# A convolution by transforms woven with a mixture of experts: gate operations spread over a step and held at the turn, spare x tiles handed out earlier, output transposes moved behind the next kind's first matmuls

## The chip, the cores and the metric

The kernel runs on one NeuronCore of a Trainium2 chip. The engines are TensorE (PE; PEld is its weight load), VectorE (DVE), ScalarE (ACT), GpSimd (POOL) and SyncE (SP). Each takes its own instructions in program order; SP, ACT and POOL also issue DMAs. The metric is the device time of one execution in microseconds (us).

## The reference, cut to what matters

```python
Xf = np.fft.rfft(x, n=2*S, axis=1); Hf = np.fft.rfft(h, n=2*S, axis=0)
y = np.fft.irfft(Xf * Hf[None], n=2*S, axis=1)[:, :S, :]     # 8 x 5056 x 128
x = y.reshape(B * S, D)
g = argmax(x @ w_group); e = argmax(x @ w_expert[g])         # 4 groups of 4 experts
out = g_w * e_w * (relu(x @ w1[g, e]) @ w2[g, e])            # F = 1024; softmax weights of the two choices
```

Every one of 8 x 5056 tokens of 128 channels is convolved along its sequence, and the result is routed to one of 16 experts.

## The kernel before, in words

**Three rounds of the convolution.** Round 0 transforms h and two sequences of x, rounds 1 and 2 three sequences each. A round has three stages. *Stage 1* (`stage1`, 96 half steps over 48 x tiles) multiplies an x tile by the matrix `f` on PE; ACT and DVE evacuate to `st`. Matmuls read x tiles from five permanent tiles `xt` and, later in the round, from four tiles `xy` that are the idle product tiles (tag `y`), zeroed by POOL in `clear` (L387). When tile i is done its buffer is free again and up to two loads (`load`, L402) are issued, from SP in round 0 and from ACT's queue in rounds 1 and 2. *Groups* (`groups`, 20 double steps a round): a step does two forward transforms (PE L520), for each two products from PSUM on DVE (`y` and `m`, L538), their sum (L572, POOL in round 0, DVE after), and two inverse transforms of the step before (PE L588), evacuated by ACT (`zs`, L598) and stored to `zd`. Forward, inverse and stage 1 take turns on three PSUM buffers `pp`. *Side* (`side`): round r's last stage and its gates run beside the later round: lumps of last transform (PE L722, L736 on `zm`, `zt` loaded from `zd`), logits (`lm`, L789; `lt`, L799), transposes of rows (`rows`, L779, evacuated by ACT as `rw`, L780), then `gate_math` on DVE (some 33 small operations, eight empty turns, and a last part with two pairs of small matmuls L972, L973, then `off`, `base`, `cs`, `posf`, L976 to L986), and scatters of rows by POOL (L855), each preceded by a cast of `pos`.

**The weave.** `run` writes rounds 0 to 2 and the experts' steps as one list `main` of (weight, function). `weave` runs it in order and lays each side's steps between by weight. A group step has eleven entries, `GW = [0, 0, 0, 0, 0, 0, 2.0, 0, 0, 0, 2.0]`, so side work falls due at its seventh and eleventh entry. A side's large steps run where they fall due. Small ones (gate operations) wait in `light` and are flushed at entries of weight 0, evenly over the run of zeros at hand (`room`): the six at a step's start or the three between the two weights. One eighth of a side takes eight units of its own time: lumps at 0 and 3, `lm` with the first rows at 4.7, `lt` with the next at 6.4, the rest of the rows (`more`) at 9.5, gate operations from 6.5 to 12.1.

**The turn and the experts.** After round 2's groups `turn` gives the PSUM and SBUF of the transforms to the experts; `ffn_first` transposes the first block's rows (L1306) and splits them and the first weights into high and low parts (L1298 on ACT, L1299 on DVE). Each block of tokens is then eight steps of `mm1` (L1351 to L1353; ACT's relu L1356, DVE's low part L1357) and `mm2` (L1369 to L1371). Round 2's last inverses stand between the first experts' steps. Blocks come in three kinds, of 512, 384 (`T0`) and 256 (`H0`) tokens; the later ones hang on counts that are known at run time (branches at L1555). Between kinds the kernel does two `mm1` of the next kind, then `ffn_drain`: the last two `mm2`, `out_evac` (ACT, `oT`, L1374), transposes of `oT` (PE, L1385), the scaled rows (DVE, L1389) and the scatter (POOL, L1422).

Of the kernel before, what the change touches and what calls it, by code (L numbers as in the profile page):

```python
# [20 lines left out]
N1, N2 = 158, 64  # L21
L = N1 * N2
NH = S // N2
# [3 lines left out]
BLK = 512  # L27
# [9 lines left out]
TB, HB = 384, 256  # L37
# [12 lines left out]
SLOTS = 56  # L50
LATE = 4
END0 = 20
SIDEG = 8
NTA = 7
FILL = 12
AHEAD = 40
# [114 lines left out]
    }  # L171


def weave(main, sides):


    light = []

    def flush(n):
        for f in light[:n]:  # L180
            f()
        del light[:n]

    room = [0] * (len(main) + 1)
    for i in reversed(range(len(main))):
        room[i] = room[i + 1] + 1 if main[i][0] == 0 else 0
    for i, (w, f) in enumerate(main):
        f()
        if w == 0:
            flush(-(-len(light) // room[i]))  # L190
        for s in sides:
            if s["start"] <= i < s["end"]:
                if i == s["start"]:
                    s["done"] = 0
                    s["acc"] = s["sacc"] = 0.0
                    s["len"] = sum(w for w, _ in main[s["start"]:s["end"]])
                    s["total"] = sum(x[0] for x in s["steps"])
                s["acc"] += w / s["len"]
                while s["done"] < len(s["steps"]) and (s["sacc"] < s["acc"] * s["total"] - 1e-6 or i == s["end"] - 1):
                    sw, sf, small = s["steps"][s["done"]]  # L200
                    if small and room[i + 1] > 0 and i < s["end"] - 1:
                        light.append(sf)
                    else:
                        if small:
                            flush(len(light))
                        sf()
                    s["sacc"] += sw
                    s["done"] += 1
                if i == s["end"] - 1:
                    flush(len(light))  # L210
# [18 lines left out]
class Kernel:  # L229
# [33 lines left out]
    def setup(self):  # L263
        nc, a, cp, dr = self.nc, self.a, self.cp, self.dr
        self.zd = [dr.tile([N1, N2, W], F32, name=f"zd{r}") for r in range(3)]
        self.hd = dr.tile([NQ, 128, 2, D], F32, name="hd")
        self.outd = dr.tile([PUT1 - PUT0, 128, 2, D], F32, name="outd")
        self.puts, self.taken = [], []
        self.srt = dr.tile([NR, ROW], F32, name="srt")
        self.tabd = [dr.tile([128, 2], I32, name=f"tabd{i}") for i in range(6)]  # L270

        self.xt = [cp.tile([128, 512], F32, name=f"xt{i}") for i in range(XT)]
        for t in self.xt:
            nc.vector.memset(t, 0.0)
        self.f = cp.tile([128, N1], F32, name="f")
        nc.sync.dma_start(out=self.f, in_=a["c_f"])

# [93 lines left out]
    def stage1(self, r):  # L371
# [21 lines left out]
        def load(eng=nc.sync):  # L393
            if asked[0] >= len(loads) or not free:
                return
            i = asked[0]
            asked[0] += 1
            u, q = loads[i]
            b = ROUNDS[r][u]
            src = a["h"] if b < 0 else a["x"][b]  # L400
            held[i] = t = free.pop(0)
            eng.dma_start(  # L402
                out=t[X0:X0 + NH + 1].rearrange("p (d n) -> p d n", n=N2), in_=src[:, 2 * q * QB:2 * (q + 1) * QB, :]
            )
            tiles[i] = t.rearrange("p (i h n) -> p i h n", h=2, n=N2)

        def mm(k):
# [34 lines left out]
            else:  # L442
                nc.scalar.copy(out=all_st[:, :, d], in_=whole.rearrange("p (i j) -> p j i", i=QB)[:, 0:N1])
            free.append(held.pop(i))
            c = i - (5 if r > 0 else 0)
            if 0 <= c < 4:
                clear()
            if 2 <= c < 6:
                free.append(cleared[c - 2])
            for _ in range(2):  # L450
                load(nc.scalar if r > 0 else nc.sync)

# [232 lines left out]
    def side(self, r):  # L685
# [131 lines left out]
        for o in range(N2 // 8):  # L817
            math = {}
            ops = self.gate_math(od, math, b0 * S + o * 8, T, nu, REST if r < 2 else REST2)
            sends = [self.scatter(math, k, GP if k < T - 1 else last, r, T) for k in range(T)]  # L820
            if r < 2:
                t = 8 * o
                at.append((t, lump(2 * o), False))
                at.append((t + 3, lump(2 * o + 1), False))
                at.append((t + 4.7, both(lm, lambda: rows(0)), False))
                at.append((t + 6.4, both(lt, lambda: rows(1)), False))
                at.append((t + 9.5, both(*more), False))
                at += [(t + 6.5 + 5.6 * k / (NMATH + REST), advance(ops), True) for k in range(NMATH + REST)]
                at.append((t + 12.15, lambda o=o, s=sends: self.sends.extend((8 * r + o, f) for f in s), True))
            else:  # L830

                t = 6 * o
                at.append((t, lump(2 * o), False))
                at.append((t + 2, lump(2 * o + 1), False))
                at.append((t + 3, both(lm, lambda: rows(0)), False))
                at.append((t + 4, both(lt, lambda: rows(1)), False))
                at.append((t + 5, both(*more), False))
                at += [(t + 4.02 + 3.3 * k / (NMATH + REST2), advance(ops), True) for k in range(NMATH + REST2)]
                at.append((t + 7.4, lambda o=o, s=sends: self.sends.extend((8 * r + o, f) for f in s), True))
# [701 lines left out]

        return [step(i) for i in range(ns)]

    def ffn_drain(self, n):
        ns = steps_of(n)
        self.mm2(n, ns - 2, 0)
        self.mm2(n, ns - 1, 0)
        self.out_evac(n, 0)
        self.out_store(n, self.lids)
        self.scatter_out(4)  # L1550

# [26 lines left out]
    def ffn_tail(self):  # L1578
# [4 lines left out]
        nt = nc.values_load(self.nbt, min_val=0, max_val=NE)  # L1583
        nh = nc.values_load(self.nbh, min_val=0, max_val=NE)
        self.ffn_chain(NW_MIN, NW_MAX, nw, NC, (BLK, self.lids))
        for i in range(2):
            self.mm1(T0, i)
        self.ffn_drain(BLK)
        self.no_rows()
        self.ffn_chain(T0, T0 + NE, nt, T0, None)  # L1590
        for i in range(2):
            self.mm1(H0, i)
        self.ffn_drain(TB)
        self.no_rows()
        self.ffn_chain(H0, H0 + NE, nh, H0, None)
        self.ffn_drain(HB)
# [1 line left out]
    def run(self):  # L1598
        tc = self.tc
        with ExitStack() as ctx:  # L1600
            self.pools(ctx)
            with ExitStack() as c2:
# [29 lines left out]
                for r in range(3):  # L1632
# [27 lines left out]
                    for p in range(0, NQ, 2):  # L1660
                        for w, f in steps[p // 2]:
                            add(f, w)
                        if p >= NQ - LOAD1:
                            add(advance(s1[r + 1][0] if r < 2 else early))
                add(turn)
                add(lambda: self.ffn_first(0))
                rest = late(2)
# [3 lines left out]
                for k, f in enumerate(steps):  # L1671
# [22 lines left out]
                    if k < 4:  # L1694
                        add(lambda q=(0, 2, 1, 3)[k]: self.ffn_w(1, (q,)))
                    add(f, FW[k % 8])
                    if k in (8 * (N0 - 2) - 1, 8 * (NA - 2) - 1):
                        add(self.drain)
                    elif k < 8 * (NA - 2) and k % 8 not in (3, 4, 5, 6):
# [7 lines left out]
                        add(lambda i=m * n // TAKE: self.take(i))  # L1707
                weave(main, [
                    dict(start=mark["start", r], end=mark["end", r], steps=side[r][1]) for r in range(3)
                ])  # L1710
                self.ffn_tail()


# [25 lines left out]
```

## Time and profile before

| | us |
|---|---|
| median of 3 runs | 1701.14 (1698.09 to 1708.59) |
| the profiled execution | 1700.13 |
| its span, first to last instruction | 1698.3 |
| PE busy in the span | 1630.5 (96%) |
| DVE, ACT, POOL busy | 1302.5, 1046.8, 773.3 |
| granted PE clock, mean | 0.991 |

The profiled execution's time is 1.8 us more than its span. The parts of the profile used below are the busy times by stretch, the waits (an engine's idle time before an instruction, put down to what came last), the timeline (start, length, engine, line, operation, idle time before it and who ended it), the groups of instructions by line, and the DMA queues (q1 is SP's, q10 is ACT's). Matmuls are pipelined, so a busy PE is not PE at its peak. A granted clock of 1 is 2.4 GHz, of 0.5 is 1.2 GHz.

### The profile page before, as it was taken

What the parts mean: (1) busy time and instruction counts of PE and PEld (TensorE: products, weight loads), DVE (VectorE), ACT (ScalarE), POOL (GpSimd) and SP (SyncE); (2) the same over time, 40 slices, a digit from 0 to 9 for tenths busy, and PEclk for the clock granted to TensorE, in tenths of its full rate; (3) what the DMA queues carried; (4) which work ended last, traced back from release to release, by engine and by line L of the source; (5) the groups of instructions that cost most, each with busy time, mean ns of one, the idle gap of its engine ahead of it and who ended that gap; (6) DMA issues with size and microseconds to landing.
All of it is one profiled execution on the core that took longest, in us unless ns stands there. A gap on an engine that the chain in (4) does not pass through costs nothing. (4 is left out here: it accounts for less than half of the span.)

```text
span 1698.3 us, 50924 instructions
## 1 busy us (share of the span) xinstructions
PE 1630.5 (96%) x18317; PEld 1275.8 (75%) x18317; DVE 1302.5 (77%) x3092; ACT 1046.8 (62%) x2461; POOL 773.3 (46%) x742
## 2 busy tenths in 40 slices
PE   8998999989899989999999999999999999999996
PEld 7676755557665557888778887888888888879986
DVE  6554698975788886777777788888887787878875
ACT  5564544544545456666666676777777776657764
POOL 1452233442555553254554454446565663334443
PEclk9999999999999999999999999999999999999998
DMA  7797678888798976566655544567555774444554
GB/s 210 224 295 223 191 243 263 274 245 217 200 289 280 287 227 172 165 177 179 177 164 173 158 139 129 153 197 219 161 161 152 213 220 139 126 132 145 164 160 139
DMA packets 278001, 330.36 MB, mean 195 GB/s; under 512 B 31863, under 2 KB 210304, under 8 KB 277720
## 3 DMA queue, kind: packets, MB, share of 16 engines
q1 hardware_dynamic: 248856, 270.93, 54.6%
q0 software_dynamic: 20608, 41.79, 7.2%
q10 hardware_dynamic: 8256, 14.10, 3.0%
q8 instruction: 152, 2.49, 0.7%
q14 instruction: 129, 1.06, 0.2%
HBM read 230.35 MB, written 96.86 MB: 193 GB/s over the span
## 5 line engine op out<-in xcount | busy, mean ns | idle before, releaser
L855 POOL DMA_INDIRECT srt<-rw,pos x320 | 345.3, 1079 | 391.4 <-DVE pos L854 116.2
L1422 POOL DMA_INDIRECT out<-orow,at x176 | 187.8, 1067 | 254.1 <-ACT at L1420 226.8
L1422 POOL DMA_INDIRECT out<-orow,sids x92 | 94.1, 1022 | 126.1 <-DVE orow L1389 89.4
L538 DVE TENSOR_TENSOR y<-pp,hg 128x768 f32<-128x768 f32 (+1 forms) x120 | 103.6, 864 | 54.3 <-ACT hg L528 32.3
L598 ACT COPY zs<-pp 128x768 f32<-128x768 f32 (+1 forms) x118 | 85.3, 723 | 81.0 <-PE pp L588 40.5
L588 PE MATMUL pp<-y,cg 64*64 64x384 f32 (+1 forms) x1472 | 116.4, 444 | 12.1 <-DVE m L538 8.0
L1357 DVE SCALAR_TENSOR_TENSOR h0l<-px,h0h 128x512 fp32r<-128x512 f32 (+1 forms) x109 | 73.7, 676 | 59.3 <-ACT h0h L1356 58.4
L520 PE MATMUL pp<-st,cg 64*64 64x192 f32 (+1 forms) x1556 | 114.4, 404 | 1.2 <-PE pp L520 0.6
L1356 ACT ACTIVATE h0h<-px 128x512 fp32r<-128x512 f32 (+1 forms) x109 | 63.9, 587 | 80.6 <-PE px L1353 72.5
L438 DVE TENSOR_TENSOR st<-pp,odd 128x320 f32<-128x320 f32 x96 | 46.9, 489 | 77.2 <-ACT odd L437 76.9
L538 DVE TENSOR_TENSOR m<-pp,hg 128x768 f32<-128x768 f32 (+1 forms) x120 | 102.9, 857 | 2.1 <-ACT hg L530 2.1
L1357 DVE SCALAR_TENSOR_TENSOR h2l<-px,h2h 128x512 fp32r<-128x512 f32 (+1 forms) x112 | 75.5, 674 | 31.0 <-ACT h2h L1356 29.9
L588 PEld LDWEIGHTS pp<-y,cg 64*64 64x64 f32 x1472 | 55.4, 133 | 52.4 <-issue 27.6
L722 PEld LDWEIGHTS py<-ig,zm 126*64 126x64 f32 x2048 | 75.0, 139 | 24.6 <-issue 8.2
L743 ACT COPY yT<-py 128x474 f32<-128x474 f32 (+1 forms) x96 | 44.3, 514 | 77.3 <-PE py L736 70.9
L1357 DVE SCALAR_TENSOR_TENSOR h3l<-px,h3h 128x512 fp32r<-128x512 f32 (+1 forms) x111 | 74.6, 672 | 22.5 <-ACT h3h L1356 21.0
L722 PE MATMUL py<-ig,zm 126*64 126x79 f32 x2048 | 83.2, 237 | 8.0 <-DMA zm<-zd 4.7
L520 PEld LDWEIGHTS pp<-st,cg 64*64 64x64 f32 x1556 | 59.0, 133 | 41.1 <-issue 32.5
L572 POOL TENSOR_TENSOR y<-y,m 128x512 f32<-128x512 f32 x40 | 50.8, 1274 | 76.8 <-DVE m L560 43.3
L1356 ACT ACTIVATE h3h<-px 128x512 fp32r<-128x512 f32 (+1 forms) x111 | 65.3, 588 | 29.1 <-PE px L1353 24.4
L1357 DVE SCALAR_TENSOR_TENSOR h1l<-px,h1h 128x512 fp32r<-128x512 f32 (+1 forms) x111 | 74.7, 673 | 4.2 <-ACT h1h L1356 0.3
L1356 ACT ACTIVATE h1h<-px 128x512 fp32r<-128x512 f32 (+1 forms) x111 | 65.2, 587 | 17.0 <-PE px L1353 14.6
(476 smaller groups left out, 5151.7 us busy)
## 6 DMA issues: line engine op xcount, KB each, us to landing
wr<-in_moe_w SPq DMA_DIRECT2D x373, 256.0 KB
zd<-zs SPq DMA_DIRECT2D x78, 384.0 KB
zm<-zd SPq DMA_DIRECT2D x64, 378.0 KB
cg<-in_c_g SPq DMA_DIRECT2D x102, 224.0 KB
xr<-srt SPq DMA_DIRECT2D x71, 260.0 KB
hg<-hd SPq DMA_DIRECT2D x80, 128.0 KB
zd<-zs SPq DMA_DIRECT2D x39, 256.0 KB
xt<-in_x ACTq DMA_DIRECT2D x54, 160.0 KB
```

The costliest lines, as they stand in the source:

```text
L438: nc.vector.tensor_tensor(out=all_st[:, 0:2 * HALF, d], in0=even, in1=odd, op=ALU.add)
L520: nc.tensor.matmul(px[c * 64:c * 64 + 64, b, to], lhsT=k, rhs=data[:, of], start=begin, stop=i == len(steps) - 1 or p == 0 and i == 1, til ...
L538: nc.vector.tensor_tensor(out=t[:, :, 0:w].rearrange("p t (r u d) -> p t r u d", r=2, u=nu), in0=taken(px, part).unsqueeze(1).broadcast_to ...
L572: (nc.gpsimd if r == 0 else nc.vector).tensor_tensor(out=y[:, :, 0:w], in0=y[:, :, 0:w], in1=m[:, :, 0:w], op=ALU.add)
L588: nc.tensor.matmul(pz[c][h:h + 64, 0:w], lhsT=wt[c * 64:c * 64 + 64, k + h:k + h + 64], rhs=y[c * 64:c * 64 + 64, part, 0:w], start=part = ...
L598: nc.scalar.copy(out=z[:, 0:n, 0:w], in_=pp[:, 0:n, 0:w])
L722: nc.tensor.matmul(pys[q][c:c + 64, col(n, u)], lhsT=zms[q][:, n % QB, k:k + 64], rhs=self.ig[:, 0:NH], start=n % QB == 0 and u == 0, stop ...
L743: nc.scalar.copy(out=self.yT[:, k:k + QB * c1], in_=pys.pop(q)[:, 0:QB * c1])
L855: ins = self.nc.gpsimd.indirect_dma_start(out=self.srt, out_offset=bass.IndirectOffsetOnAxis(ap=k["pos"][0:p, j:j + 1], axis=0), in_=k["rw ...
L1356: nc.scalar.activation(out=hh, in_=p, func=AF.Relu)
L1357: nc.vector.scalar_tensor_tensor(out=hl, in0=p, scalar=0.0, in1=hh.bitcast(F32), op0=ALU.max, op1=ALU.subtract)
L1422: ins = self.nc.gpsimd.indirect_dma_start(out=self.a["out"], out_offset=bass.IndirectOffsetOnAxis(ap=ids, axis=0), in_=o, in_offset=None, ...
```

## The change

Six edits:

- `weave`: over the convolution a zero entry's `room` is the number of zeros among the next eleven entries (nine in a group step) when that is over five, so that light operations are shared out over a whole step. From five entries ahead of `turn` to the end of the experts' second step (`hold`) none is flushed, and those that fall due are kept.
- The side's schedule in rounds 0 and 1: `lt` from 6.4 to 5.8, `more` from 9.5 to 7.4, gate operations from 6.5 to 5.9.
- Round 0's side starts two half steps of stage 1 later (`SIDEG` 8 to 10). Round 1's start stays, since `END0` is 20.
- In rounds 1 and 2 the four product tiles are zeroed at x tiles 0 to 3 and handed out at 2 to 5; before it was 5 to 8 and 7 to 10.
- The first x tile's zeroing and load are cut in two halves.
- Between kinds of blocks the two `mm1` of the next kind stand after `out_evac` and before the transposes of `oT`.

```diff
-SIDEG = 8
+SIDEG = 10
...
-def weave(main, sides):
+def weave(main, sides, turn, start):
...
+    hold = range(turn - 5, start)
+    for i in range(turn):
+        near = sum(w == 0 for w, _ in main[i:min(i + len(GW), turn)])
+        room[i] = near if near > len(GW) // 2 else room[i]
     for i, (w, f) in enumerate(main):
         f()
-        if w == 0:
+        if w == 0 and i not in hold:
             flush(-(-len(light) // room[i]))
...
-                    if small and room[i + 1] > 0 and i < s["end"] - 1:
+                    if small and (room[i + 1] > 0 or i in hold) and i < s["end"] - 1:
                         light.append(sf)
...
         for t in self.xt:
-            nc.vector.memset(t, 0.0)
+            for c in (slice(0, 256), slice(256, 512)) if t is self.xt[0] else (slice(0, 512),):
+                nc.vector.memset(t[:, c], 0.0)
...
+            n = 2 if r == 0 and i == 0 else 1
+            for c in range(n):
+                d = slice(2 * q * QB + 2 * QB // n * c, 2 * q * QB + 2 * QB // n * (c + 1))
...
-            c = i - (5 if r > 0 else 0)
-            if 0 <= c < 4:
+            if i < 4:
                 clear()
-            if 2 <= c < 6:
-                free.append(cleared[c - 2])
+            if 2 <= i < 6:
+                free.append(cleared[i - 2])
...
-                at.append((t + 6.4, both(lt, lambda: rows(1)), False))
-                at.append((t + 9.5, both(*more), False))
-                at += [(t + 6.5 + 5.6 * k / (NMATH + REST), advance(ops), True) for k in range(NMATH + REST)]
+                at.append((t + 5.8, both(lt, lambda: rows(1)), False))
+                at.append((t + 7.4, both(*more), False))
+                at += [(t + 5.9 + 5.6 * k / (NMATH + REST), advance(ops), True) for k in range(NMATH + REST)]
...
-    def ffn_drain(self, n):
+    def ffn_drain(self, n, following=None):
         ns = steps_of(n)
         self.mm2(n, ns - 2, 0)
         self.mm2(n, ns - 1, 0)
         self.out_evac(n, 0)
+        if following is not None:
+            for i in range(2):
+                self.mm1(following, i)
         self.out_store(n, self.lids)
...
-        for i in range(2):
-            self.mm1(T0, i)
-        self.ffn_drain(BLK)
+        self.ffn_drain(BLK, T0)
...
-        for i in range(2):
-            self.mm1(H0, i)
-        self.ffn_drain(TB)
+        self.ffn_drain(TB, H0)
...
+                mark["turn"] = len(main)
                 add(turn)
...
+                    if k == 1:
+                        mark["first"] = len(main)
```

## Rows read from the trace of the kernel before

**Rows 1.** The page's first part: each engine's busy us with its share of the span and its count of instructions.

```profile
PE 1630.5 (96%) x18317; PEld 1275.8 (75%) x18317; DVE 1302.5 (77%) x3092; ACT 1046.8 (62%) x2461; POOL 773.3 (46%) x742
```

**Rows 2.** Busy time by stretch, cut at the stages: round 1's groups, round 2's groups, the turn, the experts' blocks of 512. Columns: the stretch, its us, then busy us (and instructions) of PE, PEld, DVE, ACT and POOL, granted PE clock, DMA share, GB/s.

```profile
204.00:361.00 157.00, 149.31 (x2507) 89.62 (x2508) 140.13 (x338) 73.34 (x199) 59.27 (x54) 1.00 0.80 251
...
435.00:613.00 178.00, 168.43 (x3025) 107.03 (x3018) 153.31 (x386) 88.12 (x237) 103.02 (x96) 1.00 0.85 262
613.00:620.00 7.00, 5.67 (x40) 2.09 (x32) 6.81 (x17) 2.42 (x4) 3.43 (x3) 0.51 0.69 224
620.00:1524.00 904.00, 898.30 (x5658) 730.01 (x5654) 714.72 (x1575) 628.89 (x1442) 435.93 (x409) 1.00 0.58 168
```

**Rows 3.** PE's waits over the whole span: who waited for whom, us in total, times, longest us.

```profile
PE pp L588 <- DVE m L538: 8.0, 10, 2.6
...
PE py L722 <- DMA zm<-zd: 4.7, 4, 1.7
...
PE pp L419 <- DMA xt<-in_x: 3.3, 4, 1.6
PE py L722 <- ACT rw L780: 3.2, 3, 1.3
PE ptr L1385 <- ACT oT L1374: 3.2, 3, 2.1
...
PE ptr L1306 <- DVE base L977: 1.3, 1, 1.3
```

**Rows 4.** Timeline of the first 7 us: start us, us, engine, line, operation, count, idle time before it and who ended it.

```profile
1.00 2.65 DVE L274 MEMSET xt<- 128x512 f32 x5 [1.00 <-PEq L1721]
1.51 2.48 SPq L402 DMA_DIRECT2D xt<-in_h  x5
...
4.35 2.41 PE L419 MATMUL pp<-f,xt 64*64 64x80 f32 x64 [4.35 <-DMA xt<-in_h]
```

**Rows 5.** Timeline of round 1's stage 1 where its side (round 0's) starts.

```profile
148.08 4.12 SPq L702 DMA_DIRECT2D zm<-zd  x2
...
153.56 0.77 PE L722 MATMUL py<-ig,zm 126*64 126x79 f32 x16 [1.72 <-DMA zm<-zd]
```

**Rows 6.** Timeline of round 2's stage 1: x tile 9 is asked for, tiles 9 and 10 are multiplied, and the first lump of round 1's side.

```profile
371.76 0.32 ACTq L402 DMA_DIRECT2D xt<-in_x  x1
...
378.30 0.78 PE L419 MATMUL pp<-f,xt 64*64 64x80 f32 x32 [1.56 <-DMA xt<-in_x]
...
380.16 0.78 PE L419 MATMUL pp<-f,xt 64*64 64x80 f32 x32 [1.08 <-DMA xt<-in_x]
380.88 3.36 PE L722 MATMUL py<-ig,zm 126*64 126x79 f32 x48
```

**Rows 7.** DMA queues from 366 to 374 us: packets, MB, share of 16 engines.

```profile
q1 hardware_dynamic: 630, 1.14, 47.8%
q10 hardware_dynamic: 304, 0.53, 21.8%
```

**Rows 8.** Round 2's groups, 435 to 611 us, DVE's instructions by line: count, busy us, mean ns of one, idle us before and who ended it.

```profile
L538 DVE TENSOR_TENSOR y<-pp,hg 128x768 f32<-128x768 f32 x39 | 37.0, 949 | 10.4 <-PE pp L520 8.5 <-issue 1.3 <-DMA hg<-hd 0.3
L538 DVE TENSOR_TENSOR m<-pp,hg 128x768 f32<-128x768 f32 x38 | 36.0, 946 | 2.1 <-ACT hg L530 2.1
L572 DVE TENSOR_TENSOR y<-y,m 128x768 f32<-128x768 f32 x38 | 35.5, 948 | 0.0
```

**Rows 9.** PE's waits in round 1's groups alone, 204 to 361 us.

```profile
PE pp L588 <- DVE m L538: 4.5, 7, 1.2
```

**Rows 10.** ACT's waits in round 2's groups, 435 to 611 us.

```profile
ACT te L903 <- DVE td L897: 14.3, 6, 3.4
```

**Rows 11.** Timeline of one lump in round 2's groups that waits for the evacuation of transposed rows.

```profile
525.01 1.86 PE L722 MATMUL py<-ig,zm 126*64 126x79 f32 x48 [1.03 <-ACT rw L780]
```

**Rows 12.** Timeline of the turn: the products of the last group step, an inverse, ACT's evacuation of the last `pp`, the gates' last part (first and last operation), the experts' first transposes and first `mm1`, and the first low part of a hidden layer.

```profile
610.43 0.96 DVE L538 TENSOR_TENSOR y<-pp,hg 128x768 f32<-128x768 f32 x1
...
612.53 2.34 PE L588 MATMUL pp<-y,cg 64*64 64x384 f32 x16 [2.58 <-DVE m L538]
...
614.95 0.80 ACT L598 COPY zs<-pp 128x768 f32<-128x768 f32 x1 [4.04 <-issue]
...
615.89 0.16 DVE L976 TENSOR_TENSOR off<-pp,base 128x16 f32<-128x16 f32 x1
...
616.41 1.09 PE L1306 MATMUL ptr<-ident,xr 128*128 128x128 f32 x4 [1.33 <-DVE base L977]
...
617.63 0.17 DVE L986 TENSOR_TENSOR posf<-posf,sg 128x15 f32<-128x15 f32 x1
...
620.09 0.50 PE L1351 MATMUL px<-x0h,w0h 128*128 128x512 f32 x1
...
621.72 0.69 DVE L1357 SCALAR_TENSOR_TENSOR h0l<-px,h0h 128x512 fp32r<-128x512 f32 x1 [1.64 <-ACT h0h L1356]
```

**Rows 13.** Timeline of the two places between kinds of blocks: ACT's first relu of the next kind, its evacuation `oT` and PE's transposes of it at the first place, and the transposes at the second.

```profile
1528.21 0.49 ACT L1356 ACTIVATE h0h<-py 128x384 fp32r<-128x384 f32 x1 [5.20 <-PE pz L1371]
...
1528.97 0.59 ACT L1374 COPY oT<-pz 128x512 f32<-128x512 f32 x1
...
1529.62 0.66 PE L1385 MATMUL ptr<-ident,oT 128*128 128x128 f32 x4 [2.07 <-ACT oT L1374]
...
1626.32 0.79 PE L1385 MATMUL ptr<-ident,oT 128*128 128x128 f32 x3 [0.57 <-ACT oT L1374]
```

More of the change, by code (lines that the diff above doesn't have):

```diff
@@ L401, in load @@
             held[i] = t = free.pop(0)
-            eng.dma_start(
-                out=t[X0:X0 + NH + 1].rearrange("p (d n) -> p d n", n=N2), in_=src[:, 2 * q * QB:2 * (q + 1) * QB, :]
-            )
+            n = 2 if r == 0 and i == 0 else 1
+            for c in range(n):
+                d = slice(2 * q * QB + 2 * QB // n * c, 2 * q * QB + 2 * QB // n * (c + 1))
+                eng.dma_start(
+                    out=t[X0:X0 + NH + 1, 512 // n * c:512 // n * (c + 1)].rearrange("p (d n) -> p d n", n=N2),
+                    in_=src[:, d, :],
+                )
             tiles[i] = t.rearrange("p (i h n) -> p i h n", h=2, n=N2)
@@ L1709, in run @@
                     dict(start=mark["start", r], end=mark["end", r], steps=side[r][1]) for r in range(3)
-                ])
+                ], mark["turn"], mark["first"])
                 self.ffn_tail()
```

## The prediction, on record before the change was run

> **What bounds the kernel now.** I read the page's busy times first. PE is busy for 96% of the span [rows 1], so what the change could win on PE is the idle time between its instructions, some 68 us of 1698, and what a halved clock costs. The stretches come next. The experts' blocks of 512, more than half of the span, keep PE busy for 898.3 of 904 us, and no edit reaches into them. In the groups of rounds 1 and 2 PE is busy for 149.3 of 157 and 168.4 of 178 us, DVE for 140.1 and 153.3: two engines near their limit, PE ahead. At the turn the granted clock is 0.51, so most of those 7 us ran at 1.2 GHz [rows 2]. The waits then say which gaps the change can close: 8.0 us of inverses behind DVE's `m`, 4.7 behind `zm`, 3.3 behind x tiles, 3.2 behind ACT's `rw`, 3.2 behind `oT`, 1.3 behind `base` at the turn [rows 3]. That is 23.7 us together, 1.4% of the span, and no edit is aimed at more.
>
> The sum is made against the profiled execution, 1700.13 us. The median of the three runs shown is 1.0 us above it; I add that at the end.
>
> **Opening (first x tile in halves).** The tile's zeroing takes about 0.5 us (five in 2.65), its load is issued at 1.51, and PE starts at 4.35 [rows 4]. Half the zeroing lets the first half load go 0.25 us sooner. Half of 160 KB saves up to 0.38 us of transfer; that is an estimate from q1 and q10, which moved 1.67 MB in 8 us [rows 7]. The second issue, near 0.5 us on SP (five in 2.48), pushes the four other tiles back by about 0.25, which PE doesn't see, since each tile keeps it busy for over half a microsecond. I take -0.4, bounds -1.0 and +0.1.
>
> **x tiles sooner, and round 0's side later.** In round 1 the wait is not for x but 1.72 us for the side's second `zm` [rows 5]. Starting the side two half steps later gives it one tile's time, 0.78 us by the x32 in [rows 6]. Against it, four more x tiles are asked for just then on ACT's queue, and `zm` comes through SP's; 0.64 MB at the 0.21 MB/us of [rows 7] is 3.1 us of both queues, of which 1.3 could fall on `zm` if it gets its turn in more than half. I take -0.4, bounds -1.7 (the wait gone) and +1.3. POOL waits for nothing but the free product tiles there, so I cost the zeroing at nothing.
>
> In round 2 PE waits 1.56 and 1.08 us for tiles 9 and 10 [rows 6], most of its 3.3 us behind x [rows 3]. Tile 9 was asked for at 371.76 and its product starts at 378.30: 6.5 us in a queue rather than a late request [rows 6]. The new order frees a buffer at tile 2, so tiles 9 and 10 are asked for one or two tiles sooner, but into a queue that has a backlog. From 366 to 374 us q10 moved 0.53 MB beside q1's 1.14 [rows 7], so it had not an even share all the time, and I take -1.2, somewhat under half of the 2.6. The far gain is -4.8: all 3.3 behind x, and 1.5 of half clock, since the lump that follows takes 3.36 us for 48 matmuls where another takes 1.86 [rows 6, 11]. The zeroings stand between POOL's scatters now, and ACT issues these loads, so a late one holds an evacuation; one of those is 0.80 us [rows 12], and +0.8 is the other bound. By the Trainium skill, "DMA: Bandwidth & Descriptors", section on queues, rings and completion order, each DMA engine goes round the queue rows that have work, a packet at a time; a longer backlog then wins a queue no more turns, this term would be 0, and the time 1697.7. The 6.5 us of tile 9 agree with it; no row here shows the turns themselves.
>
> **Gate operations shared over a step, logits sooner, rest of the rows sooner.** DVE's work is the same; part of it moves from the three entries after the sums to the six with the products. Those products are 0.95 us each, two to a transform, and a sum [rows 8]. What can be won is PE's wait for `m`: 8.0 less 2.58 at the turn [rows 3, 12], so 5.4, of which 4.5 are in round 1 [rows 9]. What can be lost is on ACT, which takes its work in order and waits 14.3 us for DVE's `td` in round 2's groups already [rows 10], time it can't give to `rw`. And the large steps come closer. One due entry of a group step is worth 1.09 side units in round 1 (weight 2.0 of 126.6, 68.55 units) and 1.18 in round 2. `more` at 7.4 and the next lump at 8.0 are 0.6 apart, so in about half of the cases they fall on one entry; before they were 1.5 apart and never did. Of 16 eighths some 11 lie in group steps, so about five lumps stand right behind transposes whose `rw` ACT must copy first: at 1.03 us, where the trace shows that wait [rows 11], 5.2 us. I take -0.5, near nothing, because PE's whole wait for `m` in round 1 is 3% of that stretch [rows 2, 9]; bounds -5.4 and +5.2.
>
> **The turn.** The experts' transposes start at 616.41, 1.33 us after PE ran dry, because the bank of the gates' last matmuls is released by `base` [rows 12]. Held back, those matmuls take a bank of the experts. The next thing late is ACT's `zs` of the last inverse, done at 615.75, so 0.66 to 1.33 are won: -1.0. Before that an inverse waits 2.58 us for `m` [rows 12]; by my count of the entries about five gate operations that stand ahead of that step's first product now stand behind it or later, at 0.17 us each [rows 12]: -0.6. The held operations, from 615.89 to 617.80, are 1.9 us of DVE after the experts' second step; DVE is idle for 1.64 us ahead of the first low part [rows 12], and that cover leaves +0.4; without it, 1.9. Sum -1.2. If the clock stays up as well, 5.67 busy at 0.51 shrink by 2.8 [rows 2]: bounds -6.7 (1.33, 2.58 and 2.8) and +1.9.
>
> **Between kinds.** At the first place ACT starts its first relu only at 1528.21, and `oT` stands behind two relus until 1528.97. With `oT` first the transposes come 0.76 us sooner, not the whole 2.07 [rows 13]: ACT is late next. At the second place the gap is 0.57 [rows 13], but ACT's next splits now stand behind relus that come later; I count it as nothing. Sum -0.8, bounds -1.3 and +0.6 (one `oT` more on the path).
>
> **Sum.** -0.4 - 0.4 - 1.2 - 0.5 - 1.2 - 0.8 = -4.5: 1695.6 against the profiled execution, 1696.6 on the scale of the median. I predict 1696.5.
>
> **The rivals.** *Slower: lumps behind `rw`.* In the groups of rounds 1 and 2 lumps pile up behind `more`, and ACT, held by gate operations that wait for DVE, copies `rw` late, at 1.03 us a lump. The other terms give 4.0, so it decides from the fourth new wait on; at eight, 8.2 - 4.0 = +4.2, 1705.3, and at all eleven 1708.5. For it: ACT's 14.3 us behind `td` [rows 10], and `more` on one entry with a lump. Against: only three such waits, 3.2 us, stand in the trace [rows 3]. Chance 0.2.
>
> *More: the clock stays up.* If `m` and x come in time, the halved clock after each gap goes too, 1.5 and 2.8 us as worked out above, and 4 of the 5.4 behind `m` in place of 0.5: 1696.6 - 4.3 - 3.5 = 1688.8. For it: both halved stretches follow a gap [rows 6, 12]. Against: only part of each gap is removed. Chance 0.18.
>
> *Nothing moves.* The x tiles come no sooner, since the queue is full, what the turn saves is paid in the experts' first steps, and the rest can't be told from nothing: 1699.5 to 1701. Chance 0.14. The forecast has 0.48, its own range 1692 to 1699.
>
> **How the numbers follow.** About 1% is what a measurement of this kernel tells from no change: 17 us, under 1684.1 or over 1718.2. All bounds on one side give -21 or +9.9; neither end is likely whole. The range 1687 to 1706 takes in the second rival's time and most of the first's. Faster by over 1% needs nearly every bound at once, 0.05; slower by over 1% a wait that no row shows, 0.03.
>
> **What would show it.** PE's first matmul before 4.2 us; the wait for `zm` in round 1 under 1.4, on x in round 2 under 2; waits for `m` in the groups below 5.4 and for `rw` not above 5; the experts' transposes right behind the last inverse's evacuation; the first wait for `oT` near 1.3. I am wrong if the groups' stretches, 157 and 178 us, change by more than 3 us either way, or if a halved clock comes or goes.

## The result and the profile after

The changed kernel takes 1714.21 us (1706.73 to 1720.31), beside 1703.36 us for the kernel before on the same chip: a ratio of 1.0062 with a 95% interval of 1.0043 to 1.0081. A second set of runs (e6 below) gives 1.0083 [1.0056, 1.0111]. The forecast was 1696.5 with a range to 1706.0; the time came out above the range, on the other side of no change. The profiled execution took 1706.73 us, the fastest of its runs, with a span of 1704.9 against 1698.3.

Engine busy, the row that answers to [rows 1], and then the busy time by stretch, cut where a PE instruction starts that both kernels have: round 1's groups, round 2's groups, from the turn to the last `mm2` ahead of the first place between kinds, that place up to the third `mm1` of the next kind, the second place in the same way, and from there to the end. (Line numbers here are 8 higher than before: the products are L546, the inverses L596, the lumps L730, `rw` L788.)

```profile
PE 1631.0 (96%) x18317; PEld 1276.4 (75%) x18317; DVE 1299.5 (76%) x3096; ACT 1045.6 (61%) x2458; POOL 772.2 (45%) x742
```

```profile
211.62:367.23 155.61, 145.33 (x2370) 85.30 (x2368) 134.82 (x317) 71.56 (x194) 54.09 (x50) 1.00 0.78 250
453.76:624.52 170.76, 157.36 (x2707) 97.57 (x2707) 146.30 (x356) 80.61 (x222) 96.65 (x88) 1.00 0.85 263
...
624.52:1530.94 906.42, 901.37 (x5677) 732.28 (x5678) 719.35 (x1590) 629.84 (x1444) 440.95 (x414) 1.00 0.57 169
1530.94:1537.81 6.87, 5.12 (x19) 3.93 (x17) 1.00 (x4) 1.19 (x3) 0.00 (x0) 0.75 0.58 163
...
1627.72:1632.93 5.21, 3.13 (x23) 2.81 (x23) 0.83 (x5) 1.08 (x2) 0.00 (x0) 1.00 0.37 99
1632.93:1704.90 71.97, 58.97 (x459) 56.38 (x457) 50.13 (x129) 42.23 (x88) 31.18 (x29) 0.93 0.52 159
```

The same stages of the kernel before, cut in the same way (the cuts of [rows 2] were rounder):

```profile
210.18:361.45 151.27, 144.52 (x2363) 85.32 (x2361) 136.04 (x319) 71.10 (x194) 57.17 (x52) 1.00 0.82 258
447.43:616.41 168.98, 158.08 (x2712) 97.70 (x2711) 148.36 (x360) 81.37 (x223) 98.08 (x91) 0.99 0.86 267
616.41:1523.36 906.95, 901.51 (x5674) 731.50 (x5674) 717.63 (x1581) 630.51 (x1445) 437.35 (x411) 1.00 0.58 168
1523.36:1530.03 6.67, 3.47 (x18) 2.51 (x17) 1.63 (x6) 1.35 (x3) 0.00 (x0) 1.00 0.61 169
...
1619.88:1626.87 6.99, 4.57 (x24) 3.74 (x23) 2.23 (x7) 2.28 (x5) 0.00 (x0) 0.76 0.25 75
1626.87:1698.30 71.43, 58.30 (x458) 56.21 (x456) 48.82 (x126) 41.11 (x86) 31.20 (x29) 0.93 0.53 161
```

PE's work is the same to half a microsecond. The two groups' stages are 4.3 and 1.8 us longer, and almost all of that is idle PE: span less busy is 10.28 against 6.75 us in round 1, 13.40 against 10.90 in round 2. From the turn to the end the change is 1.5 us shorter, nearly all of it at the two places between kinds, 12.1 us together against 13.7. So the change wins a little at the end and loses in the groups. In the second pair of profiles (e5, e6) the spans differ by 14.1 us, of which the two groups' stages are 11.1. Which wait grew is told by PE's waits over the whole span, the rows that answer to [rows 3]:

```profile
PE py L730 <- ACT rw L788: 9.7, 7, 2.3
...
PE pp L596 <- DVE m L546: 8.6, 9, 1.9
...
PE pp L428 <- DMA xt<-in_h: 3.3, 1, 3.3
...
PE py L1022 <- DVE nba_m L1017: 2.3, 1, 2.3
...
PE py L730 <- DMA zm<-zd: 1.0, 2, 0.7
PE ptr L1314 <- ACT zs L606: 1.0, 1, 1.0
PE pp L428 <- DMA xt<-in_x: 0.9, 1, 0.9
...
PE ptr L1393 <- ACT oT L1382: 0.5, 1, 0.5
```

The waits for `zm` (4.7 to 1.0), x (3.3 to 0.9, and a new 0.7 through `xy`) and `oT` (3.2 to 0.5) are nearly gone. The wait for `m` stayed, and the one for ACT's `rw` tripled, from 3.2 us in 3 to 9.7 in 7. The timeline of round 2's groups shows one of them. Read it by engine: PE transposes rows, then wants the lump L730, whose bank those rows occupy until ACT has copied them.

```profile
517.97 0.98 PE L787 MATMUL py<-ident,yT 128*128 128x128 f32 x7
518.02 0.95 DVE L580 TENSOR_TENSOR y<-y,m 128x768 f32<-128x768 f32 x1
...
518.95 0.95 DVE L580 TENSOR_TENSOR y<-y,m 128x768 f32<-128x768 f32 x1
...
520.06 0.22 DVE L905 TENSOR_TENSOR td<-lg,tmx 128x60 f32<-128x60 f32 x1
520.32 0.25 ACT L911 ACTIVATE te<-td 128x60 f32<-128x60 f32 x1 [0.97 <-DVE td L905]
...
520.61 0.97 ACT L788 COPY rw<-py 128x512 f32<-128x512 f32 x2
...
521.25 1.86 PE L730 MATMUL py<-ig,zm 126*64 126x79 f32 x48 [2.29 <-ACT rw L788]
```

The transposes end at 518.95. ACT is busy until 519.35; its next instruction is a gate operation, `te`, which waits 0.97 us for DVE's `td`, and DVE has two sums of 0.95 us and a small operation to do first. So `rw` starts at 520.61, and with the copy itself PE stands for 2.29 us. Beside it the same lump in the kernel before, the one of [rows 11]:

```profile
520.24 0.98 PE L779 MATMUL py<-ident,yT 128*128 128x128 f32 x7
...
522.50 1.15 PE L520 MATMUL pp<-st,cg 64*64 64x384 f32 x16
...
523.00 0.80 ACT L598 COPY zs<-pp 128x768 f32<-128x768 f32 x1 [2.70 <-DMA zd<-zs]
...
524.07 0.22 ACT L956 CAST tot<-cs 128x16 bf16<-128x16 f32 x1 [0.18 <-DVE cs L938]
...
524.37 0.97 ACT L780 COPY rw<-py 128x512 f32<-128x512 f32 x2
```

ACT was even later there, 3.2 us behind the end of the transposes (521.2 to 524.37), held by `zs` and by another gate operation. But PE had two forward transforms to do in between, 521.15 to 523.98, and stood for 1.03 us only. In the trace of before no lump stands right behind such transposes ahead of the turn; in this one four do, with nothing between. Those four waited 2.34, 1.33 (in the lump's middle), 2.29 and 0.76 us, 6.7 together; the other three waits in the row are 3.0.

### The profile page after: what moved, and what is told of

Its sections match the earlier page's. It is cut to its first block, busy times and chain, and to the rows that moved or that the text cites. A ratio compares the mean times of both kernels' runs of the same rounds, so it can differ in the third digit from the quotient of the medians.

```text
span 1704.9 us, 50911 instructions
## 1 busy us (share of the span) xinstructions
PE 1631.0 (96%) x18317; PEld 1276.4 (75%) x18317; DVE 1299.5 (76%) x3096; ACT 1045.6 (61%) x2458; POOL 772.2 (45%) x742
## 5 line engine op out<-in xcount | busy, mean ns | idle before, releaser
L546 DVE TENSOR_TENSOR y<-pp,hg 128x768 f32<-128x768 f32 (+1 forms) x120 | 103.7, 864 | 66.7 <-ACT hg L536 31.0
L596 PE MATMUL pp<-y,cg 64*64 64x384 f32 (+1 forms) x1472 | 115.6, 442 | 10.4 <-DVE m L546 8.6
L546 DVE TENSOR_TENSOR m<-pp,hg 128x768 f32<-128x768 f32 (+1 forms) x120 | 103.0, 858 | 4.3 <-ACT hg L538 4.2
L596 PEld LDWEIGHTS pp<-y,cg 64*64 64x64 f32 x1472 | 55.3, 133 | 50.9 <-issue 28.6
L730 PEld LDWEIGHTS py<-ig,zm 126*64 126x64 f32 x2048 | 73.3, 137 | 26.5 <-ACT rw L788 12.5
L730 PE MATMUL py<-ig,zm 126*64 126x79 f32 x2048 | 81.2, 235 | 10.9 <-ACT rw L788 9.7
L428 PE MATMUL pp<-f,xt 64*64 64x80 f32 x2208 | 58.9, 244 | 18.0 <-issue 9.0
```

The lines of the kernel that those rows point to most:

```text
L428: nc.tensor.matmul(pp[c * 64:c * 64 + 64, b, j * 2 * HALF:(j + 1) * 2 * HALF], lhsT=tiles[i][b * 64:b * 64 + 64, j, c, :], rhs=self.f[b * ...
L546: nc.vector.tensor_tensor(out=t[:, :, 0:w].rearrange("p t (r u d) -> p t r u d", r=2, u=nu), in0=taken(px, part).unsqueeze(1).broadcast_to ...
L596: nc.tensor.matmul(pz[c][h:h + 64, 0:w], lhsT=wt[c * 64:c * 64 + 64, k + h:k + h + 64], rhs=y[c * 64:c * 64 + 64, part, 0:w], start=part = ...
L730: nc.tensor.matmul(pys[q][c:c + 64, col(n, u)], lhsT=zms[q][:, n % QB, k:k + 64], rhs=self.ig[:, 0:NH], start=n % QB == 0 and u == 0, stop ...
```

## The experiments

Two theories stood against each other: that the side's new schedule (`lt` 5.8, `more` 7.4, gate operations 5.9) puts transposes of rows right ahead of lumps; and that the sharing of gate operations over a step, or the hold, delays something. The other edits (x tiles and `SIDEG`, halves, the drain between kinds) were the third suspects.

**First round (e1 to e4): the gates' edits apart.** Kernel e1 is the change without sharing and schedule, e2 is the kernel before with both, e3 with the schedule alone, e4 with the sharing alone.

```diff
# e3; e2 has this and the sharing
-                at.append((t + 6.4, both(lt, lambda: rows(1)), False))
-                at.append((t + 9.5, both(*more), False))
-                at += [(t + 6.5 + 5.6 * k / (NMATH + REST), advance(ops), True) for k in range(NMATH + REST)]
+                at.append((t + 5.8, both(lt, lambda: rows(1)), False))
+                at.append((t + 7.4, both(*more), False))
+                at += [(t + 5.9 + 5.6 * k / (NMATH + REST), advance(ops), True) for k in range(NMATH + REST)]
# e4; e1 has neither
+    for i in range(turn):
+        near = sum(w == 0 for w, _ in main[i:min(i + len(GW), turn)])
+        room[i] = near if near > len(GW) // 2 else room[i]
```

> The change without the sharing of gate operations and without the side's new schedule (lt, more and the gate operations at their old times); the hold at the turn, x tiles sooner, round 0's side later, the halved first tile and the transposes' new place stay. Theory 1 (the cost is in the side's schedule: the rest of the rows stands right ahead of a lump, which waits for ACT's rw): 0 to 5 us faster than before, waits of lumps for rw back at about 3 us. Theory 2 (the cost is in the sharing: gate operations between the products hold up m and ACT): the same as theory 1 here. Theory 3 (the cost is outside the groups: opening, experts' first steps, between kinds): 6 to 10 us slower than before.

> Before with the sharing and the side's new schedule alone. Theories 1 and 2: 6 to 11 us slower than before, lumps wait for rw 8 us or more. Theory 3: within 2 us of before.

> Before with lt at 5.8, the rest of the rows at 7.4 and the gate operations from 5.9, without sharing. Theory 1: 5 to 8 us slower, lumps wait for rw 8 us or more. Theory 2: within 2 us of before, waits for rw about 3 us. Theory 3: within 2 us.

> Before with the gate operations shared over a step, at the old times of the side's schedule. Theory 1: 0 to 3 us faster than before, waits for m down. Theory 2: 5 to 8 us slower, waits for m or rw up. Theory 3: within 2 us.

Measured: 1.0067 [1.0041, 1.0092], 1.0109 [1.0087, 1.0131], 1.0148 [1.0121, 1.0174] and 1.0076 [1.0048, 1.0103]. These four ran on a chip on which the kernel before itself took 1786 us, so their ratios are read against one another only. On that chip each of the four is slower than before, the schedule alone most, 0.7% above the sharing alone. That points to the schedule, but e1, which has neither, was expected faster by both theories and is slower too. Where all edits cost something it settles nothing; the parts were run again on other chips.

**Both kernels again (e5, e6).** The kernel before and the changed one, unedited, for a second profile of each.

> The kernel before itself, for its stages and waits on the same chip as the other runs of this call. Every theory: the time of before.

> The changed kernel itself beside the parts. Theories 1 and 2 (the cost is in the groups, by the schedule or by the sharing): 0.3 to 0.8% slower than before, lumps wait for rw 5 us more than in before. Theory 4 (each edit costs a little wherever it is, because the order before was fitted to what late deliveries there are): slower too, with the loss spread over stage 1, the groups and the experts. A rival to all: no difference on this chip.

Measured: 1699.73 us, and 1713.68 against 1700.67, 1.0083 [1.0056, 1.0111]. The loss is real. The second profile of the change shows more of what a late `rw` costs. This is the lump that in the first profile (227.16, after a wait of 2.34) took 1.31 us, and the stretch that follows it:

```profile
231.04 2.38 PE L730 MATMUL py<-ig,zm 126*64 126x79 f32 x32 [2.34 <-ACT rw L788]
```

```profile
230.50:237.50 7.00, 6.46 (x92) 5.02 (x96) 0.69 (x4) 1.64 (x6) 1.67 (x2) 0.52 0.54 146
```

The same wait, and this time the granted clock was 0.52 for the next 7 us: 6.46 busy us, which at full clock would be about 3.4 (an estimate, 6.46 x 0.52). The price of such a wait is thus 2.3 us, and sometimes 2.3 and some 3 more.

**Hold alone, and x alone (e7, e8).** The kernel before with `hold` only; the kernel before with the x tiles sooner and `SIDEG` 10 only.

```diff
# e7
-        if w == 0:
+        if w == 0 and i not in hold:
...
-                    if small and room[i + 1] > 0 and i < s["end"] - 1:
+                    if small and (room[i + 1] > 0 or i in hold) and i < s["end"] - 1:
# e8
-            c = i - (5 if r > 0 else 0)
-            if 0 <= c < 4:
+            if i < 4:
...
-SIDEG = 8
+SIDEG = 10
```

> Before with the hold at the turn alone, neither sharing nor the new schedule. Theory 3 (the cost is outside the groups): 1 to 3 us slower: the transposes at the turn come sooner by 1 us, but the table's matmul in the experts' first steps waits 1.5 us longer and the clock may fall behind it. Theories 1 and 2: within 2 us of before. Theory 4: 3 to 8 us slower.

> Before with x tiles handed out sooner and round 0's side two half steps later, nothing else. Theories 1 and 2: within 2 us of before, the wait for x in round 2 from 3 to 1 us. Theory 4: 3 to 8 us slower, lost in stage 1 of rounds 1 and 2.

Measured: 0.9995 [0.9979, 1.0010] and 0.9999 [0.9981, 1.0016]. Neither gains nor costs anything that shows. With e8 the wait for x in xt falls from 3.3 to 1.2 us, but a tile read through `xy` now waits 2.9: the wait changed its place.

**Rows sooner alone, sharing alone, all but the schedule, all but the gates (e9 to e12).** One edit against its absence, on one chip.

```diff
# e9, the kernel before with
-                at.append((t + 9.5, both(*more), False))
+                at.append((t + 7.4, both(*more), False))
# e10 is e4's kernel, e12 is e1's; e11 is the change with the three old times
```

> Before with the rest of the rows (more) at 7.4 in place of 9.5, nothing else: they stand right ahead of the next lump. Theory 1: 4 to 8 us slower, lumps wait for rw 7 us or more, the groups of rounds 1 and 2 longer by 4 us or more together. Theory 2: within 2 us of before.

> Before with the sharing alone, again, since the run before it was on a chip on which the kernel before itself took 1786 us. Theory 1: within 3 us of before, to either side; waits of lumps for rw 3 us. Theory 2: 5 to 8 us slower.

> The change with lt, the rest of the rows and the gate operations at their old times. Theory 1: 0 to 4 us faster than before, waits of lumps for rw near 3 us. Theory 2: 5 us or more slower than before. Theory 4: 5 us or more slower.

> The change without sharing and without the new schedule, again, beside before on this chip. Theories 1 and 2: 0 to 4 us faster than before. Theory 4: 6 to 12 us slower, as on the chip on which before took 1786 us.

Measured: 1.0098 [1.0075, 1.0122], 0.9975 [0.9958, 0.9991], 0.9996 [0.9973, 1.0019], 1.0000 [0.9983, 1.0016]. One number in the kernel before, `more` from 9.5 to 7.4, loses as much as the whole change does, or more; the change without its schedule loses nothing; sharing alone gains a quarter of a per cent. In e9 five lumps stand right behind transposes of rows; they waited 3.26, nothing, 0.44, 2.32 and 0.35 us. Its two groups, and two of these lumps:

```profile
214.60:371.46 156.86, 146.22 (x2366) 86.79 (x2363) 136.99 (x320) 72.70 (x196) 57.55 (x53) 0.99 0.79 251
458.00:632.60 174.60, 159.89 (x2712) 99.68 (x2711) 148.56 (x360) 80.92 (x223) 98.13 (x91) 0.99 0.85 260
```

```profile
230.70 1.31 PE L722 MATMUL py<-ig,zm 126*64 126x79 f32 x32 [3.26 <-ACT rw L780]
...
521.85 0.98 PE L779 MATMUL py<-ident,yT 128*128 128x128 f32 x7
525.16 2.94 PE L722 MATMUL py<-ig,zm 126*64 126x79 f32 x48 [2.32 <-ACT rw L780]
```

After the 2.32 us the 48 matmuls take 2.94 us where [rows 11] has 1.86, at a halved clock again. The groups' stages are 5.6 us longer than before's in each round.

In e10 PE waits for `m` once in round 1's groups and once in round 2's (a row each), where [rows 9] had 4.5 us in 7 for round 1 alone:

```profile
PE pp L591 <- DVE m L541: 1.3, 1, 1.3
...
PE pp L591 <- DVE m L541: 2.5, 1, 2.5
```

**Other places for the rows, and the parts that gain (e13 to e16).** e13 is the change with `more` at 6.9, half a unit further ahead of the lump. e14 is the kernel before with `more` at 6.9, 0.5 behind `lt`. e15 is the kernel before with `more` at 8.6, 0.6 behind a lump. e16 is the kernel before with sharing, hold and the drain between kinds, on the old schedule.

```diff
# e13 (in the change) and e14 (in the kernel before)
+                at.append((t + 6.9, both(*more), False))
# e15 (in the kernel before)
+                at.append((t + 8.6, both(*more), False))
# e16: the lines of e4 and e7, and
+        if following is not None:
+            for i in range(2):
+                self.mm1(following, i)
```

> The change with the rest of the rows at 6.9 in place of 7.4: 1.1 ahead of the next lump and 1.1 behind lt. If the place right ahead of a lump is the cause: within 0.25% of before or faster, lumps wait for rw 4 us or less, no lump or one right behind a transpose of rows. If sooner rows cost wherever they are: 0.5% slower or more.

> Before with the rest of the rows at 6.9 alone: 1.1 ahead of the lump, 0.5 behind lt (6.4) and its rows. If the lump behind the rows is the cause: within 0.3% of before. If any pile of large steps on one entry costs: 0.5% to 1% slower, as with 7.4.

> Before with the rest of the rows at 8.6 alone: 0.6 behind a lump, so in half of the cases right behind it on one entry, 2.4 ahead of the next. If the lump that waits for rw is the cause: within 0.3% of before. If any pile on one entry costs: 0.5% to 1% slower.

> Before with the sharing, the hold at the turn and the transposes' new place, at the old schedule, without the x tiles, the later side and the halved tile. Parts taken singly gave -0.25% (sharing) and 0 (hold): 0.2 to 0.5% faster than before if they add up; within 0.15% if the sharing's gain was chance or the hold gives it back in the experts' first steps.

Measured: 1.0004 [0.9989, 1.0020], 1.0051 [1.0029, 1.0073], 1.0012 [0.9995, 1.0030] and 0.9955 [0.9939, 0.9971]. Half a unit earlier, and the change's loss is gone. Behind the lump the rows cost nothing measurable, though transposes wait 5.0 us there for ACT's `yT`. Piled on `lt` in the kernel before they cost half a per cent with no wait of a lump for `rw`: there it is the transposes themselves that wait, 3.2 us for ACT's `lg`. So e14 came out as the rival theory had it, that any pile of large steps on one entry costs, and e15 did not; neither theory alone covers both. e16, 1694.25 against 1701.71, beats both kernels. Its groups' stages:

```profile
213.12:363.57 150.45, 144.66 (x2369) 85.68 (x2365) 134.24 (x315) 70.83 (x194) 55.32 (x50) 1.00 0.81 259
448.77:613.00 164.23, 156.59 (x2708) 97.58 (x2707) 145.51 (x353) 80.53 (x220) 94.22 (x88) 1.00 0.88 273
```

The groups of rounds 1 and 2 together, from the stretches and PE's waits inside them (us):

| | stages | PE busy | PE idle | wait for `m` | lump's wait for `rw` |
|---|---|---|---|---|---|
| before | 320.2 | 302.6 | 17.6 | 7.9 | 3.2 |
| before again (e5) | 319.1 | 301.6 | 17.5 | 8.6 | 3.8 |
| change | 326.4 | 302.7 | 23.7 | 8.6 | 8.4 |
| change again (e6) | 330.2 | 306.0 | 24.2 | 9.1 | 9.1 |
| hold only (e7) | 321.3 | 303.1 | 18.2 | 9.7 | 4.5 |
| x and side (e8) | 319.9 | 304.5 | 15.4 | 5.9 | 5.3 |
| rows sooner only (e9) | 331.5 | 306.1 | 25.4 | 10.6 | 6.4 |
| sharing only (e10) | 315.1 | 301.0 | 14.1 | 3.8 | 3.2 |
| all but schedule (e11) | 316.2 | 301.2 | 15.0 | 5.0 | 6.0 |
| all but gates (e12) | 319.5 | 302.3 | 17.2 | 6.4 | 6.4 |
| change, rows at 6.9 (e13) | 327.4 | 308.1 | 19.3 | 8.4 | 2.4 |
| before, rows at 6.9 (e14) | 328.7 | 305.2 | 23.6 | 9.8 | 0 |
| before, rows at 8.6 (e15) | 322.9 | 302.3 | 20.6 | 10.2 | 0 |
| share, hold, drain (e16) | 314.7 | 301.2 | 13.4 | 3.8 | 4.3 |

Five things are in it.

- The two profiles with `more` at 7.4 and the sharing (change, e6) have 6 to 7 us more idle PE than before, of which 5.2 and 5.3 are `rw`.
- These waits don't tell a kernel's time by themselves. In e9 they are 3.2 us of 7.8 more idle; e11 and e12 have 6.0 and 6.4 of them and lose nothing; e14 has none, and as much idle PE as the change. The runs show that `more` at 7.4 is the cause: it loses alone (e9), and at the old schedule, or with 6.9, the loss is gone (e11, e13). That lumps waiting for `rw` are the way from it to the loss is seen for most of the change's idle time, and argued for the rest.
- Where the clock halved behind such a wait, 3 to 4 us of PE's busy time come on top (e6, e9). It did so behind three of the six waits of some 2.3 us or more that change, e6 and e9 have behind transposes.
- Where the x tiles are not handed out sooner, the sharing takes the wait for `m` from 7.9 to 9.7 us down to 3.8; beside that edit only from 5.9 and 6.4 to 5.0. Under the new schedule it stands at 8.4 to 9.1, whether the lumps collide or not. So what the sharing saves of this wait is not seen there. Why `m` is late under the new schedule was not isolated.
- e13's profile, at its median time, has groups as long as the change's (327.4 against 326.4), so the profiles don't show where the half unit saves its time. Nor was it isolated why its PE is busy 6.9 us longer than e16's; two halved stretches lie in its groups, which is only about half of that.

The gains don't add up either. e11 is e16 with the x tiles, the later side and the halved tile, and stands at 0.9996 [0.9973, 1.0019] where e16 stands at 0.9955 [0.9939, 0.9971], on another chip. Edits that cost nothing alone (e8) seem to cost 0.4% in this company; no run isolates it. Gate operations alone at 5.9 with the rows left at 9.5 were not tried.

## Why the prediction was wrong

**Gate operations shared, rows sooner: the step that failed.** The text had the parts: about five lumps right behind transposes, `rw` late because ACT is held by operations that wait for `td`, bounds of -5.4 and +5.2. The count held (four, and five in e9). Two things did not. The price of a wait was mis-sized: it was taken as 1.03 us from [rows 11], and that row is no price: it is what was left of a delay of 3.2 us in ACT's queue after PE had done transforms beside it. With the lump right behind the transposes that cover of 2.8 us is gone: a wait is up to 2.3 us, in e9 3.3, and the four such lumps waited 6.7 us in all, 1.7 each, before the halved clock that followed in e6 and e9. And the term was set "near nothing" by a reason that has no weight here, that the wait for `m` is 3% of a stretch: this bounds the gain of the sharing, not the loss by the schedule. Two edits of opposite sign stood in one term. (Two small sums are off, by too little to matter: 2.0 of 126.6 is 1.08 of 68.55 units, not 1.09, and at the turn 1.9 less 1.64 leaves 0.3, not 0.4.) Apart they measure -0.25% (e10, -4 us, close to the -5.4 end) and, the rows alone, +0.98% (e9, +16 us, three times the +5.2 end). Their sum, +0.73%, is about what the whole change measures, 1.0062 and 1.0083; without the schedule it stands at 0.9996 (e11).

**The rival came nearest.** "Lumps behind `rw`" had the place and the waits right, and a chance of 0.2. Its time, 1705.3 at eight waits and 1708.5 at eleven, was short, for the same price of 1.03: at the four that came, 4.1 less the other terms' 4.0, it would have been no loss at all. And these waits are not the whole of it, as e9 and e14 show. The prediction's own signs, `m` in the groups below 5.4, `rw` not above 5, no stretch of the groups changed by more than 3 us, all failed: `m` in the groups is 6.7 without the 1.9 at the turn, `rw` 9.7, and round 1's stretch grew by 4.3.

**Opening.** PE starts at 3.33 in this profile, the far bound of -1.0, not -0.4. Over the five profiles with the halved tile it starts at 3.3 to 3.9, over the nine without it, outside the slow chip of e1 to e4, at 4.1 to 4.4, so -0.6 in the mean, and the -1.0 is partly luck. The load is issued at 1.28, 0.23 sooner, as worked out; from there to PE's first matmul it is 2.05 us, not 2.84, so the half load saves 0.8 here where I estimated up to 0.38. Whether the gain reaches the end doesn't show: round 1 begins at 139.98, before's at 139.16.

**x tiles and the side.** Both waits fell as forecast: for `zm` in round 1's stage 1 from 1.72 us to 1.0 in two, for x in round 2 to 0.9, and 0.7 more through `xy`. Cut at the stages' first PE instructions, the two stretches are not shorter (71.6 against 71.0, 86.5 against 86.0), and e8 alone is 0.9999. Where the gaps went, in rounds 1 and 2:

```profile
150.83 0.78 PE L428 MATMUL pp<-f,xt 64*64 64x80 f32 x32 [1.68 <-DVE st L448]
...
380.06 1.21 PE L428 MATMUL pp<-f,xt 64*64 64x80 f32 x32 [0.94 <-DMA xt<-in_x]
382.78 2.38 PE L435 MATMUL pp<-f,xy 128*64 128x158 f32 x16 [1.51 <-issue]
```

One gap of 1.7 us behind DVE's evacuation and one of 1.5 for which the profile shows no releaser ("issue") took their place. Over the whole span such gaps ahead of stage 1's matmuls grew from 7.5 to 12.2 us. Terms of -0.4 and -1.2 were gaps that the next thing refilled; taken alone, 0 was the right value. By the rule of the Trainium skill that the prediction weighed ("DMA: Bandwidth & Descriptors", queues, rings and completion order) the term for round 2 was 0 as well, but for another reason, that a longer backlog wins no turns. The wait for x fell by 2.4 us, so the tiles did come sooner: the runs agree with that value, and not with the reason.

**The turn.** The steps came as worked out: the experts' transposes stand behind ACT's `zs` of the last inverse, and the inverse waits 1.91 for `m`, not 2.58 [rows 12].

```profile
622.05 1.52 PE L596 MATMUL pp<-y,cg 64*64 64x384 f32 x16 [1.91 <-DVE m L546]
624.52 0.66 PE L1314 MATMUL ptr<-ident,xr 128*128 128x128 f32 x4 [0.95 <-ACT zs L606]
...
635.54 0.17 PE L1022 MATMUL py<-nba_m,ones 128*128 128x16 bf16 x1 [2.34 <-DVE nba_m L1017]
```

```profile
636.00:640.00 4.00, 4.00 (x13) 3.04 (x12) 2.55 (x13) 1.70 (x3) 0.00 (x0) 0.57 0.97 295
```

The last two of these rows are what was missed. The gates' results feed a small table (`nba_m`) whose matmul stands in PE's queue behind the experts' third step; with the operations held, PE waits 2.3 us for it where it waited 0.8, and in this profile the halved clock that stood at the turn (613 to 620, 0.51) comes here. In e6 the same wait, 2.31 us, is followed by full clock:

```profile
644.37 0.17 PE L1022 MATMUL py<-nba_m,ones 128*128 128x16 bf16 x1 [2.31 <-DVE nba_m L1017]
...
644.50:648.50 4.00, 4.00 (x21) 3.35 (x21) 2.92 (x13) 2.29 (x4) 0.00 (x0) 1.00 0.96 270
```

The prediction costed the held operations on DVE and named their cover there, but not who waits for what they compute. In the sum it hardly shows: from the turn to the first place between kinds the change takes 906.4 us where before takes 907.0, and hold alone (e7) is 0.9995.

**Between kinds.** Forecast -0.8, at most -1.3. The transposes at the first place now have no wait at all, but PE stands at the branch for 1.27 and 0.48 us, where it stood 1.13, and the last `mm2` behind it run at a halved clock (0.75 over the 6.87 us above):

```profile
1532.60 0.51 PE L1377 MATMUL pz<-h2h,w3h 128*128 128x512 f32 x1 [1.27 <-ACTq L1566]
1533.59 0.50 PE L1378 MATMUL pz<-h2h,w3l 128*128 128x512 f32 x1 [0.48 <-DVEq L1566]
...
1535.15 0.63 PE L1379 MATMUL pz<-h3l,w3h 128*128 128x512 f32 x1
...
1537.45 0.60 PE L1393 MATMUL ptr<-ident,oT 128*128 128x128 f32 x4
```

The wait of 2.07 us went whole: the relu that I held to be "late next" starts at 1536.83, behind PE's own matmuls, and PE goes on without it. Yet the first place takes 6.87 us, not less than the 6.67 of before; in e11, e12 and e16, with the same order and no halved clock there, it takes 5.3 to 5.5. The second, which I counted as nothing, fell from 6.99 to 5.21, partly because its halved clock (0.76) did not come again. Behind it the tail is 0.5 longer. Together that is -1.0 us, near the forecast, by other steps than those worked out. Over all profiles outside the slow chip the two places take 10.1 to 12.1 us with this edit and 11.8 to 13.7 without, and the tail 71.4 to 72.0 against 69.9 to 71.5.

**The rest of the numbers.** "The clock stays up" (1688.8) and "nothing moves" fell with the schedule. e16 shows what the parts that gain are worth without x tiles and without the schedule: 0.9955, -7.5 us, more than the forecast and less than this rival. The clock is part of it: 1.00 from 608 to 620 us, where the turn now lies, and 0.994 in the mean against 0.991.

## What to carry to other kernels

When a bundle of edits shares one term, price each by itself before they are set off against each other: here a gain of 4 us and a loss of 16 were written down as "near nothing". A wait read from a trace is what its cover left over, not a price: if the change moves the two ends together, add the work that stood between them back (here two transforms, 2.8 us), and read the delay from the other engine's queue (`te` behind `td` behind two sums). And of operations held back, ask who reads their results, not only whether their engine is idle.

## What the runs showed of the hardware

The clock does not answer to the same gap in the same way each time: a wait of 2.34 us ahead of the same lump was followed by full clock in one profile of the change (1.31 us for 32 matmuls) and by 7 us at 0.52 in another (2.38 us).

Chips differ by 5% on this one-core kernel. On one, the kernel before took 1786 us; elsewhere its median was 1700 to 1703. The change without sharing and schedule was profiled on that chip (e1) and on another (e12). Its row for the lumps in each (line, operation, count, busy us, mean ns of one, idle before and who ended it):

```profile
L727 PE MATMUL py<-ig,zm 126*64 126x79 f32 x2048 | 97.3, 241 | 22.1 <-issue 18.6 <-ACT rw L785 3.0
```

```profile
L727 PE MATMUL py<-ig,zm 126*64 126x79 f32 x2048 | 81.5, 235 | 8.8 <-ACT rw L785 6.4 <-DMA zm<-zd 2.4
```

Same count, nearly the same mean duration, but 18.6 us of idle time that no wait explains, and 16 us more of busy time, which is matmuls following one another more slowly. The clock (0.980 against 0.990) accounts for about a sixth of the difference in span, 17 of 97 us if all time went by it, an estimate. Why the chip differs stays open. The edits were also worth something else there: the same two kernels stand at 1.0067 and 1.0076 on that chip (e1, e4), and at 1.0000 and 0.9975 on another (e12, e10).
